# Combinations of weight quarters move from GpSimd to VectorE, lower parts of weights move from VectorE to GpSimd

## The chip, the core and the metric

The kernel runs on one core of a Trainium2 chip. The metric is device time in microseconds (us) for one execution; smaller is better. A profile of one execution shows what each engine did: TensorE (PE, with its weight loads PEld), VectorE (DVE), ScalarE (ACT), GpSimd (POOL) and the queue on SyncE (SP) that issues DMAs.

## The reference

Attention within chunks of 64 tokens, and behind it a feed-forward layer with a gate. All arrays are float32.

```python
# q, k, v: (8, 8, 576, 64); w_in: (512, 2048); w_out: (2048, 512)
scores = scale * np.matmul(q_c, k_c.transpose(0, 1, 2, 4, 3))   # chunks of 64
scores = scores - np.max(scores, axis=-1, keepdims=True)
attn = np.exp(scores)
attn = attn / (np.sum(attn, axis=-1, keepdims=True) + 1e-09)
x = matmul(attn, v_c) as (4608, 512)
h = x @ w_in
g = h * np.clip(h + 3.0, 0.0, 6.0) / 6.0
out = g @ w_out
```

## The kernel before

**Precision.** TensorE multiplies fp32r operands. Each float32 operand is split in two: an upper part (a ScalarE copy that rounds to fp32r) and a lower part (operand minus upper part). `passes` (L341 to L345) makes a product of three matmuls: upper by upper, upper by lower, lower by upper. So each tensor that TensorE reads costs one ScalarE copy and one subtraction; here these are called the upper and the lower part.

**Weights.** They arrive as 64-bit words and are decoded in 16 tiles (a0 to a7 of w_in, b0 to b7 of w_out; 128 x 1024 elements each): two ScalarE steps, a shift and a join on VectorE (L187, L194), the upper part `high` (L199, ScalarE), the lower part `lower` (L202, VectorE).

**Blocks.** The 4608 tokens are nine blocks of 512. Block 0 runs plainly (steps a, b: first product; c: second product). The other eight go in four pairs, and each pair multiplies in a scheme of seven products instead of eight on quarters of the matrices. For the first pair, half of the first product is still done plainly (steps a16 to b43 of TensorE), and the other half as seven products for each of four columns, `f1.0.4` to `f4.0.7` in the order 1, 5, 6, 7, 2, 3, 4 (the last number is the column). The second products follow as `s0.0`, `s0.1` and so on.

**Sums of weight quarters.** Four of the seven products need combinations of quarters of the weights. They are made once, 16 times (u = 0 to 15; u below 8 is w_out, u from 8 is w_in) by `sum_steps` (L426): `whole` puts two weight rows together in a tile `a` (VectorE, L442, or, for the weights kept in DRAM, a DMA, L439), `comb` makes the four combinations (L447: four operations of 128 x 256, each on all of two inputs in SBUF), `top` the upper part (L452, ScalarE), `less` the lower part (L455, VectorE, 128 x 1024), `send` four DMAs to DRAM (L460). There are two tiles `a`, so `whole` of u+2 waits for `less` of u. `own` (L466) sends the quarters that need no combination, three DMAs each. The products f5, f6, f7 and f3 of column 4 use the sum u = 12 straight from SBUF; columns 5, 6, 7 use 13, 14, 15. The sums 8 to 11 come last, during the second product.

**Operands of the first pair.** `x0.s0`, `x0.s0c`, `x0.s1` (VectorE) and `x0.s2`, `x0.s2b`, `x0.s3`, `x0.s3b` (GpSimd, L565) combine quarters of the attention's result; each is split by a ScalarE copy (L569) and a lower part (L572).

**Attention.** A head half (named by block and half, as 20, 21, 30) has scores, max, less, exp, sum, share, turn, product, keep and rest. On most, one ScalarE instruction makes all exponentials and VectorE subtracts the maximum and sums (L246, L253). For those listed in `ROWS` (L44), ScalarE makes the exponentials row by row with bias and sum in the same instruction (L265), and VectorE only negates the maxima and inverts the sums. Where a product of one head half and the scores of the next share their place, they are issued as one step.

**Order.** `Schedule` (L59) decides all of it before anything is emitted: each step has an engine, a cost in us written beside it, the steps before it and a due time. `order` (L81) plays the steps through with these costs, and each engine's queue is emitted in the order that came out. On the chip every engine works its queue strictly in this order: an instruction that waits holds all behind it.

Of the kernel before, what the change touches and what calls it, by code (L numbers as in the profile page):

```python
# [9 lines left out]
F32 = mybir.dt.float32  # L10
# [5 lines left out]
ALU = mybir.AluOpType  # L16
# [10 lines left out]
NCT, NFT, NET = DM // P, DFF // P, DO // P  # L27
# [5 lines left out]
NPL = 4  # L33
# [7 lines left out]
WARM = 12  # L41
FILL = (2.0, 4.0)
LAG = 2
ROWS = ["40", "41"]  # L44
XDVE = ["x0.s0c"]
APART = 2
EDGE = 32
HASTE = 5.0
# [4 lines left out]
PART = STEP / 4  # L53
SECOND = STEP * (17 + 2 * NPL) + PART * 7 * (NFP - NPL)
STEPS = SECOND - PART * 7 * (NFP - NPL)
COMBS = [u for u in range(16)]


class Schedule:  # L59
# [67 lines left out]
def tile_kernel(ctx: ExitStack, tc: tile.TileContext, qk_in, v_in, weights, out):  # L127
# [40 lines left out]
    words, w = {}, {}  # L168
# [10 lines left out]
    def convert(i):  # L179
        t = {}  # L180

        def upper_bits():
            t["u"] = wu.tile([P, 1024], I32, name="u")
            ACT.activation(out=t["u"].bitcast(F32), in_=words[i][:, :, 1].bitcast(F32), func=AF.Prelu, scale=2.0 ** -112, alpha=2.0 ** 32)

        def shift():
            DVE.tensor_scalar(out=t["u"], in0=t["u"], scalar1=3, scalar2=None, op0=ALU.logical_shift_left)  # L187

        def lower_bits():
            t["r"] = wr.tile([P, 1024], I32, name="r")  # L190
            ACT.activation(out=t["r"], in_=words[i][:, :, 0].bitcast(U32), func=AF.Copy, scale=2.0 ** -29)

        def join():
            DVE.tensor_tensor(out=t["u"], in0=t["u"], in1=t["r"], op=ALU.add)  # L194
            t["a"] = t["u"].bitcast(F32).rearrange("p (f t) -> p f t", f=2)

        def high():
            w[i] = w_tile(i, F32R)
            ACT.copy(out=w[i][:, :, 0], in_=t["a"])  # L199

        def lower():
            DVE.tensor_tensor(out=w[i][:, :, 1], in0=t["a"], in1=w[i][:, :, 0].bitcast(F32), op=ALU.subtract)  # L202
# [224 lines left out]
    def sum_steps(m, p):  # L427
# [26 lines left out]
        def lower():  # L454
            DVE.tensor_tensor(out=t["hl"][:, :, :, 1], in0=t["s"], in1=t["hl"][:, :, :, 0].bitcast(F32), op=ALU.subtract)  # L455

        def send():
            for i, row, col in ((5, 1, 1), (7, 1, 0), (6, 0, 0), (3, 0, 1)):
# [39 lines left out]
    def next_slot(s, name, until, stream=False):  # L498
# [8 lines left out]
            slots[0] = 0  # L507
        before = work.take(f"slot{k}", 1, name, until)
        if len(work.rings[f"slot{k}"]) == 1:
            before = [f"f4.0.{2 * (k % 4) + 1}", *owns(k)]  # L510
        return k, before

    owns = lambda k: [f"own{NFP + (2 * k + q) % NFP}" for q in range(2)]
# [3 lines left out]
    def x_steps(s):  # L517
        n = NSTD + 2 * s
        b = lambda i, j: xraw[n + j][:, i]
        name = lambda i: f"x{s}.{i}"  # L520
        minus = lambda to, x, y: lambda: DVE.tensor_tensor(out=b(*to), in0=b(*x), in1=b(*y), op=ALU.subtract)
        sub = ("DVE", 1.22)
        ops[s] = {}
        last = name("s0")
        steps = [(last, *sub, [], minus((0, 1), (0, 1), (0, 0)), [0, 1])]

        def high(i, slot):
            ops[s][i] = w_tile(f"a{slot}", F32R)
# [5 lines left out]
        for i in ORDER_A:  # L534
# [3 lines left out]
            for k, at, to, x, y, reads in (("s1", 5, (0, 1), (1, 1), (0, 1), [2]), ("s2", 6, (0, 0), (0, 1), (0, 0), []),  # L538
                                           ("s3", 6, (0, 1), (1, 0), (0, 1), [3])):
                if i == at:  # L540
                    steps.append((name(k), *sub, [name(f"{i}l"), name("1l"), last], minus(to, x, y), reads))
                    last = name(k)
        return steps

# [165 lines left out]
    for k, i in enumerate(ORDER_W):  # L710
# [4 lines left out]
        work.add(f"down{i}", "ACT", 1.15, [f"w{i}", free("join")], down)  # L715
        work.add(f"join{i}", "DVE", 1.22, [f"shift{i}", f"down{i}"], join)
        work.add(f"high{i}", "ACT", 1.05, [f"join{i}"], high)
        work.add(f"lower{i}", "DVE", 1.22, [f"high{i}"], lower)
        if i in KEPT:
            work.add(f"keepw{i}", "SP", 1.57, [f"join{i}"], keep, first=LOADS.index("w" + ORDER_W[min(k + 4, NFT - 1)]) + 0.5)  # L720

# [106 lines left out]
    for u in [*range(NFP), *range(NFP + NPL, 2 * NFP), *range(NFP, NFP + NPL)]:  # L828
# [6 lines left out]
        work.add(f"comb{u}", *(("POOL", 3.2, [f"whole{u}"], lambda f=combine: f(POOL)) if u in COMBS else ("DVE", 1.70, [f"whole{u}"], lambda f=combine: f(DVE))))  # L835
# [108 lines left out]
    def add_units(s):  # L944
# [14 lines left out]
        for i in ORDER_B:  # L959
            for pp in range(NFP // 2):  # L960
# [8 lines left out]
                def top(i=i, pp=pp, src=src, slot=slot):  # L969
# [147 lines left out]
```

## Time and profile before

| | |
|---|---|
| median of three runs | 791.15 us (790.48 to 791.26) |
| the profiled execution, its own time | 792.07 us |
| its span from first to last instruction | 790.3 us |
| TensorE busy | 775.2 us (98%) |
| VectorE busy | 634.1 us (80%) |
| ScalarE busy | 388.6 us (49%) |
| GpSimd busy | 174.9 us (22%) |
| DMA, mean | 251 GB/s |

The profiled execution took 1.8 us more than its span, and 0.9 us more than the median. Busy shares are averages over stages that differ: in the slices of 20 us, GpSimd is idle in most of the first 100 us, and busy 19.45 of 20 us between 160 and 180 us. TensorE is busy in every slice from 200 us on, save the end.

### The profile page before, as it was taken

What the parts mean: (1) busy time and instruction counts of PE and PEld (TensorE: products, weight loads), DVE (VectorE), ACT (ScalarE), POOL (GpSimd) and SP (SyncE); (2) the same over time, 40 slices, a digit from 0 to 9 for tenths busy, and PEclk for the clock granted to TensorE, in tenths of its full rate; (3) what the DMA queues carried; (4) which work ended last, traced back from release to release, by engine and by line L of the source; (5) the groups of instructions that cost most, each with busy time, mean ns of one, the idle gap of its engine ahead of it and who ended that gap; (6) DMA issues with size and microseconds to landing.
All of it is one profiled execution on the core that took longest, in us unless ns stands there. A gap on an engine that the chain in (4) does not pass through costs nothing.

```text
span 790.3 us, 14001 instructions
## 1 busy us (share of the span) xinstructions
PE 775.2 (98%) x5603; PEld 635.6 (80%) x5603; DVE 634.1 (80%) x726; ACT 388.6 (49%) x531; POOL 174.9 (22%) x139
## 2 busy tenths in 40 slices
PE   8999998989999999999999999999999999999998
PEld 4788887767888878888888888888888888888887
DVE  6999979788999779858998786687988657679851
ACT  4988843544666653433744433435643423356330
POOL 0000025799570500322300002221100013222000
PEclk9999999999999999999999999999999999999999
DMA  9999997785649898556676886576656665566572
GB/s 371 407 403 336 331 347 268 275 298 178 251 160 335 292 364 316 186 190 241 210 256 223 260 267 210 186 256 235 212 190 219 219 213 187 189 208 203 197 232 102
DMA packets 69424, 198.05 MB, mean 251 GB/s; under 512 B 7024, under 2 KB 19568, under 8 KB 65008
## 3 DMA queue, kind: packets, MB, share of 16 engines
q1 hardware_dynamic: 69216, 197.03, 72.7%
q8 instruction: 44, 0.72, 0.4%
q14 instruction: 20, 0.16, 0.1%
q10 hardware_dynamic: 144, 0.13, 0.0%
HBM read 153.09 MB, written 44.04 MB: 249 GB/s over the span
## 4 chain that ended last, share of the span: by engine, by line
PE 83%; DVE 6%; DMA 3%; POOL 3%; ACT 2%; issue 1%; SPq 1%; DVEq 0%; POOLq 0%; ACTq 0%
PE acc L343 19%; PE acc L344 19%; PE acc L345 19%; PE h L343 7%; PE h L345 7%; PE h L344 7%; POOL a L447 2%; PE two L235 2%; PE two L285 2%; DVE hl L455 1%; PE h L311 1%; DVE a L442 1%; DMA wa<-b 1%; DMA a<-wa 1%; DMA b<-wb 1%
## 5 line engine op out<-in xcount | busy, mean ns | idle before, releaser
L343 PE MATMUL acc<-wa,ws 128*128 128x512 f32 (+1 forms) x536 | 209.5, 391 | 0.1
L345 PE MATMUL acc<-wa,ws 128*128 128x512 f32 (+1 forms) x536 | 207.9, 388 | 0.0
L344 PE MATMUL acc<-wa,ws 128*128 128x512 f32 (+1 forms) x536 | 207.8, 388 | 0.0
L974 DVE TENSOR_TENSOR wa<-wb,wa 128x1024 fp32r<-128x1024 f32 x96 | 128.6, 1349 | 30.3 <-ACT wa L971 29.8
L971 ACT CAST wa<-wb 128x1024 fp32r<-128x1024 f32 x96 | 100.5, 1053 | 99.8 <-PE acc L345 63.7
L343 PEld LDWEIGHTS acc<-wa,ws 128*128 128x128 f32 x536 | 100.7, 188 | 21.7 <-DVE u L864 0.9
L345 PEld LDWEIGHTS acc<-wa,ws 128*128 128x128 f32 x536 | 100.6, 188 | 20.8
L344 PEld LDWEIGHTS acc<-wa,ws 128*128 128x128 f32 x536 | 100.7, 188 | 19.8
L938 POOL TENSOR_TENSOR wb<-wb 128x512 f32<-128x512 f32 x24 | 32.0, 1331 | 374.7 <-DVE wb L752 374.7
L447 POOL TENSOR_TENSOR a<-a 128x256 f32<-128x256 f32 x64 | 67.0, 1049 | 165.5 <-DMA b<-wb 111.0
L749 ACT ACTIVATE r<-acc,half 128x512 f32<-128x512 f32 x90 | 61.2, 686 | 39.9 <-DVE acc L864 36.6
L749 ACT ACTIVATE r<-h,half 128x512 f32<-128x512 f32 x38 | 26.1, 687 | 103.4 <-DVE h L864 98.4
L752 DVE SCALAR_TENSOR_TENSOR wb<-r,acc 128x512 f32<-128x512 f32 x90 | 60.8, 680 | 7.9 <-ACT r L749 7.9
L345 PE MATMUL h<-wa,ws 128*128 128x512 f32 (+1 forms) x144 | 55.2, 383 | 0.0
L344 PE MATMUL h<-wa,ws 128*128 128x512 f32 (+1 forms) x144 | 55.2, 383 | 0.0
L343 PE MATMUL h<-wa,ws 128*128 128x512 f32 (+1 forms) x144 | 55.2, 383 | 0.0
L864 DVE TENSOR_TENSOR u<-h,p 128x512 f32<-128x512 f32 x32 | 22.0, 689 | 27.3 <-PE h L345 27.1
L864 DVE TENSOR_TENSOR acc<-acc,u 128x512 f32<-128x512 f32 x48 | 33.0, 696 | 9.8 <-PE acc L345 9.7
L940 POOL TENSOR_TENSOR g<-wb,wb 128x512 f32<-128x512 f32 x24 | 37.8, 1577 | 1.9
L752 DVE SCALAR_TENSOR_TENSOR wb<-r,h 128x512 f32<-128x512 f32 x38 | 25.9, 682 | 12.9 <-ACT r L749 12.9
L343 PE MATMUL acc<-wa,wa 128*128 128x512 f32 x88 | 34.9, 397 | 0.5 <-DMA wa<-b 0.5
L345 PE MATMUL acc<-wa,wa 128*128 128x512 f32 x88 | 34.3, 390 | 0.0
(199 smaller groups left out, 1428.8 us busy)
## 6 DMA issues: line engine op xcount, KB each, us to landing
ws<-b SPq DMA_DIRECT2D x84, 512.0 KB, 4.6
ws<-a SPq DMA_DIRECT2D x72, 512.0 KB, 4.4
qk<-qk_in SPq DMA_DIRECT2D x17, 1024.0 KB, 7.8
wa<-b SPq DMA_DIRECT2D x28, 512.0 KB, 6.4
a<-wa SPq DMA_DIRECT2D x40, 256.0 KB, 5.8
v<-v_in SPq DMA_DIRECT2D x17, 512.0 KB, 5.5
wa<-w_in_out SPq DMA_DIRECT2D x8, 1024.0 KB, 13.0
wb<-w_in_out SPq DMA_DIRECT2D x8, 1024.0 KB, 10.3
```

What stands on the lines that cost most here:

```text
L235: PE.matmul(self.s[o, a, c, :], lhsT=self.qk[rows, 0, c, o], rhs=self.qk[rows, 1, c, o], start=True, stop=True)
L343: PE.matmul(ps, lhsT=a_h, rhs=b_h, start=first, stop=False, skip_group_check=more)
L344: PE.matmul(ps, lhsT=a_h, rhs=b_l, start=False, stop=False, skip_group_check=more)
L345: PE.matmul(ps, lhsT=a_l, rhs=b_h, start=False, stop=last, skip_group_check=more)
L447: engine.tensor_tensor(out=to, in0=x, in1=y, op=op)
L749: ACT.activation(out=t["r"], in_=ps(), func=AF.Relu, bias=half, scale=1.0 / 6.0)
L752: work.add("gate" + name, "DVE", 0.69, ["relu" + name, *more], lambda: DVE.scalar_tensor_tensor(out=out(), in0=t["r"], scalar=1.0, in1=ps( ...
L864: return lambda: DVE.tensor_tensor(out=out(), in0=x(), in1=y(), op=ALU.add)
L938: work.add(id_("t1."), "POOL", 1.45, [id_("gate3."), id_("gate2.")], lambda f=gq: POOL.tensor_tensor(out=f(0, 1), in0=f(0, 1), in1=f(0, 0) ...
L940: work.add(id_("t2."), "POOL", 1.45, [id_("t1."), id_("gate7.")], lambda f=gq, p=p: POOL.tensor_tensor(out=t2_of(p), in0=f(1, 1), in1=f(0, ...
L971: ACT.copy(out=g_ops[s, i, pp][:, :, 0], in_=src())
L974: work.add(low, "DVE", 1.22, [high], lambda i=i, pp=pp, src=src: DVE.tensor_tensor(out=g_ops[s, i, pp][:, :, 1], in0=src(), in1=g_ops[s, i ...
```

## The change

The list of sums whose `comb` runs on GpSimd, `COMBS`, shrinks from all 16 to 8 to 11; the other twelve go to VectorE. Their lower parts `less0s` to `less7s` go from VectorE to GpSimd (`LESS_ON_POOL`), and so do the lower parts of the decoded weights b2 to b7 (`LOWER_ON_POOL`). `ROWS` gets the head halves 30 and 31. The play-through lengthens a VectorE step of the kinds in `BOTH` by 0.6 of the time that it overlaps GpSimd's current step. `XPOOL` and `ULPOOL` are empty, so the lines with them change nothing, and the new condition in `next_slot` gives the same step for every slot that comes to it. The planned cost of `comb` on GpSimd is 4.2 instead of 3.2.

```diff
-ROWS = ["40", "41"]
+ROWS = ["30", "31", "40", "41"]
+SHARED = 0.6
+BOTH = ("lower", "join", "whole", "less", "comb", "share", "glow", "ul", "m0", ...)
+LESS_ON_POOL = list(range(8))
+LOWER_ON_POOL = [f"b{i}" for i in range(2, 8)]
-COMBS = [u for u in range(16)]
+COMBS = [8, 9, 10, 11]
...
                     end = now + self.steps[n][1]
+                    if engine == "DVE" and n.startswith(BOTH):
+                        end += SHARED * max(0.0, min(end, free.get("POOL", 0.0)) - now)
...
-        def lower():
-            DVE.tensor_tensor(out=w[i][:, :, 1], in0=t["a"], in1=w[i][:, :, 0].bitcast(F32), op=ALU.subtract)
+        def lower(engine):
+            engine.tensor_tensor(out=w[i][:, :, 1], in0=t["a"], in1=w[i][:, :, 0].bitcast(F32), op=ALU.subtract)
...
-        work.add(f"lower{i}", "DVE", 1.22, [f"high{i}"], lower)
+        work.add(f"lower{i}", *(("POOL", 2.5, [f"high{i}"], lambda f=lower: f(POOL)) if i in LOWER_ON_POOL else ...))
...
-        work.add(f"comb{u}", *(("POOL", 3.2, [f"whole{u}"], ...) if u in COMBS else ("DVE", 1.70, ...)))
+        work.add(f"comb{u}", *(("POOL", 4.2, [f"whole{u}"], ...) if u in COMBS else ("DVE", 1.70, ...)))
-        work.add(f"less{u}s", "DVE", 1.22, [f"top{u}"], lower, due=due)
+        work.add(f"less{u}s", *(("POOL", 2.5, [f"top{u}"], lambda f=lower: f(POOL)) if u in LESS_ON_POOL else ...), due=due)
```

GpSimd's queue at its start. Before, the combinations of sums 0 to 6 in tiles `a`, then a part of the operands of the first pair (`wb7`):

```order
L447 TENSOR_TENSOR a_1325<-a_1325 128x256 x4
L447 TENSOR_TENSOR a_1376<-a_1376 128x256 x4
L447 TENSOR_TENSOR a_1443<-a_1443 128x256 x4
L447 TENSOR_TENSOR a_1549<-a_1549 128x256 x4
L447 TENSOR_TENSOR a_1589<-a_1589 128x256 x4
L447 TENSOR_TENSOR a_1632<-a_1632 128x256 x4
L447 TENSOR_TENSOR a_1733<-a_1733 128x256 x4
L565 TENSOR_TENSOR wb7_1792<-wb3_1432,xb_834 128x1024
```

Now the lower parts of b2 to b7 come first (two are shown), then `less0s` to `less5s` (`hl`), and `less6s` behind the first two of the `wb7` steps:

```order
L210 TENSOR_TENSOR wb6_1221<-u_1095,wb6_1221 128x2x512
L210 TENSOR_TENSOR wb7_1232<-u_1074,wb7_1232 128x2x512
L463 TENSOR_TENSOR hl_1343<-a_1295,hl_1343 128x4x256
L463 TENSOR_TENSOR hl_1408<-a_1317,hl_1408 128x4x256
L463 TENSOR_TENSOR hl_1531<-a_1432,hl_1531 128x4x256
L463 TENSOR_TENSOR hl_1594<-a_1448,hl_1594 128x4x256
L463 TENSOR_TENSOR hl_1642<-a_1564,hl_1642 128x4x256
L463 TENSOR_TENSOR hl_1757<-a_1656,hl_1757 128x4x256
L574 TENSOR_TENSOR wb7_1783<-wb3_1406,xb_832 128x1024
L574 TENSOR_TENSOR wb7_1783<-xc_1086,wb3_1406 128x1024
L463 TENSOR_TENSOR hl_1824<-a_1759,hl_1824 128x4x256
```

Every instruction on GpSimd in this place is now one of 1024 columns.

VectorE's queue before the scores of head half 21, which need `x0.s0` (`wb3`) and the rest of head half 20 (`xa`). Before, with `less0s` (`hl`) and the lower part of block 0's gate (`g2`) between them, then a gate and the `whole` of sum 2:

```order
L332 TENSOR_TENSOR xa_1393<-two_1343,xa_1393 128x2x8x64
L455 TENSOR_TENSOR hl_1405<-a_1325,hl_1405 128x4x256
L376 TENSOR_TENSOR g2_1414<-r_1294,g2_1414 128x512
L561 TENSOR_TENSOR wb3_1432<-two_1343,xb_834 128x2x8x64
L752 SCALAR_TENSOR_TENSOR wb0_1395<-r_1430,h_1328 128x512
L442 TENSOR_TENSOR a_1443<-wb1_578 128x512
L442 TENSOR_TENSOR a_1443<-wb5_1179 128x512
```

Now, with the two combinations (L455) of sums 0 and 1 ahead:

```order
L455 TENSOR_TENSOR a_1295<-a_1295 128x256 x4
L384 TENSOR_TENSOR g1_1333<-r_1251,g1_1333 128x512
L455 TENSOR_TENSOR a_1317<-a_1317 128x256 x4
L761 SCALAR_TENSOR_TENSOR wb0_1388<-r_1385,h_1267 128x512
L570 TENSOR_TENSOR wb3_1406<-two_1352,xb_832 128x2x8x64
L340 TENSOR_TENSOR xa_1402<-two_1352,xa_1402 128x2x8x64
L384 TENSOR_TENSOR g2_1422<-r_1298,g2_1422 128x512
L450 TENSOR_TENSOR a_1432<-wb1_578 128x512
L450 TENSOR_TENSOR a_1432<-wb5_1126 128x512
L761 SCALAR_TENSOR_TENSOR wb0_1388<-r_1435,h_1335 128x512
```

`x0.s0` and the rest stand ahead of `g2`, and the last gate has moved behind the `whole` of sum 2.

SyncE's queue: the sends (`own`) of the last two w_in rows (a6, a7 in DRAM) and the store of the decoded b7 (`wb7`) before, down to the last send that frees `wb3` and so `x0.s0`:

```order
L466 DMA a6_0_144<-wa3_644 128x2x256
L466 DMA a6_1_145<-wa3_644 128x2x256
L466 DMA a6_1_145<-wa7_1114 128x2x256
L205 DMA wb7_123<-u_1130 128x1024
L466 DMA a7_0_146<-wa3_644 128x2x256
L466 DMA a7_1_147<-wa3_644 128x2x256
L466 DMA a7_1_147<-wa7_1114 128x2x256
L466 DMA b1_1_149<-wb2_674 128x2x256
```

Now, from the store of b7 on:

```order
L213 DMA wb7_123<-u_1074 128x1024
L474 DMA b1_0_148<-wb1_578 128x2x256
L474 DMA b2_0_156<-wb5_1126 128x2x256
L474 DMA b4_0_158<-wb5_1126 128x2x256
L474 DMA b1_1_149<-wb2_656 128x2x256
L474 DMA b2_1_157<-wb6_1221 128x2x256
L474 DMA b4_1_159<-wb6_1221 128x2x256
L474 DMA b1_1_149<-wb3_783 128x2x256
```

The six DMAs of a6 and a7 have gone behind the sends of `wb3`.

## Rows read from the trace of the kernel before

**Rows 1.** Busy time by engine (and count), clock, DMA share, GB/s, by stretch.

```profile
120.00:140.00 20.00, 18.50 (x145) 15.56 (x146) 19.35 (x23) 7.56 (x10) 10.96 (x12) 1.00 0.81 273
160.00:180.00 20.00, 16.84 (x71) 13.19 (x70) 17.94 (x16) 9.52 (x13) 19.45 (x12) 0.96 0.81 277
```

**Rows 2.** Instructions in order of time (start, duration): TensorE, scores of 21.

```profile
121.50 1.16 PE L235 MATMUL two<-qk 64*64 64x64 f32 x64 [2.72 <-issue]
122.59 0.50 PE L343 MATMUL h<-xb,wa 128*128 128x512 f32 x1
```

**Rows 3.** The chain that ended last (start, duration), before `x0.s0`.

```profile
113.42 0.72 SPq L466
...
114.19 5.12 DMA b<-wb
...
120.19 1.21 DVE wb L561
```

**Rows 4.** TensorE in order of time, step b32 and the next.

```profile
150.03 0.50 PE L344 MATMUL h<-xd,wa 128*128 128x512 f32 x1 [0.33 <-DVE xd L332]
...
151.29 0.39 PE L343 MATMUL acc<-xa,wa 128*128 128x512 f32 x1
151.52 0.39 PE L344 MATMUL acc<-xa,wa 128*128 128x512 f32 x1
```

**Rows 5.** TensorE in order of time, first column of the seven products.

```profile
170.33 0.39 PE L343 MATMUL acc<-xb,wa 128*128 128x512 f32 x1
...
178.04 0.50 PE L343 MATMUL acc<-wa,hl 128*128 128x512 f32 x1 [3.03 <-DVE wb L752]
...
182.48 1.04 PE L285 MATMUL two<-ident,e 128*128 128x128 f32 x8
184.43 0.50 PE L343 MATMUL acc<-xd,hl 128*128 128x512 f32 x1 [0.91 <-DVE g L864]
...
185.92 0.39 PE L343 MATMUL acc<-wa,wa 128*128 128x512 f32 x1
```

**Rows 6.** VectorE in order of time, from the scores of 21 on.

```profile
121.32 0.67 DVE L752 SCALAR_TENSOR_TENSOR wb<-r,h 128x512 f32<-128x512 f32 x1
121.92 1.28 DVE L442 TENSOR_TENSOR a<-wb 128x512 f32<-128x512 f32 x2
...
127.53 1.21 DVE L253 TENSOR_REDUCE z<-e 128x16 f32<-128x1024 f32 x1
...
135.04 2.37 DVE L442 TENSOR_TENSOR a<-wb 128x512 f32<-128x512 f32 x2
...
148.68 1.29 DVE L332 TENSOR_TENSOR xd<-acc,xd 128x512 fp32r<-128x512 f32 x2 [1.22 <-ACT xd L328]
...
162.88 1.18 DVE L254 TENSOR_SCALAR z<-z 128x16 f32<-128x16 f32 x1
...
172.31 3.41 DVE L273 TENSOR_TENSOR e<-e,z 128x1024 f32<-128x1024 f32 x1
```

**Rows 7.** GpSimd in order of time, `x0.s2b`.

```profile
161.61 2.41 POOL L565 TENSOR_TENSOR wb<-wb,xb 128x1024 f32<-128x1024 f32 x1
```

**Rows 8.** Groups by line and form: busy, mean ns | idle before.

```profile
L447 POOL TENSOR_TENSOR a<-a 128x256 f32<-128x256 f32 x64 | 67.0, 1049 | 165.5 <-DMA b<-wb 111.0 <-DVE u L864 26.3 <-DVE a L442 9.1
...
L455 DVE TENSOR_TENSOR hl<-a,hl 128x1024 fp32r<-128x1024 f32 x16 | 24.0, 1500 | 7.9 <-ACT hl L452 7.3 <-DMA a<-hl 0.5
L452 ACT CAST hl<-a 128x1024 fp32r<-128x1024 f32 x16 | 16.8, 1050 | 26.6 <-POOL a L447 19.2 <-DMA a<-wa 3.9 <-DVE wb L752 2.8
...
L265 ACT ACTIVATE e<-two,m 128x64 f32<-128x64 f32 x32 | 9.7, 326 | 2.0 <-PE acc L345 1.8 <-DVE m L259 0.2
L202 DVE TENSOR_TENSOR wb<-u,wb 128x1024 fp32r<-128x1024 f32 x8 | 9.7, 1220 | 0.2 <-ACT wb L199 0.2
...
L265 ACT ACTIVATION_READ_ACCUMULATOR e<-two,m 128x1 f32 x32 | 7.0, 218 | 0.0
```

**Rows 9.** The page's DMA issues: count, KB each, median us to landing.

```profile
a<-wa SPq DMA_DIRECT2D x40, 256.0 KB, 5.8
```

More of the change, by code (lines that the diff above doesn't have):

```diff
@@ L43 @@
 LAG = 2
-ROWS = ["40", "41"]
+ROWS = ["30", "31", "40", "41"]
 XDVE = ["x0.s0c"]
+SHARED = 0.6
+BOTH = ("lower", "join", "whole", "less", "comb", "share", "glow", "ul", "m0", "m1", "m2", "m3", "x0.", "x1.", "x2.", "x3.")
+LESS_ON_POOL = list(range(8))
+XPOOL = []
+ULPOOL = []
+LOWER_ON_POOL = [f"b{i}" for i in range(2, 8)]
 APART = 2
@@ L452, in high, with lower @@
             ACT.copy(out=t["hl"][:, :, :, 0], in_=t["s"])
-        def lower():
-            DVE.tensor_tensor(out=t["hl"][:, :, :, 1], in0=t["s"], in1=t["hl"][:, :, :, 0].bitcast(F32), op=ALU.subtract)
+        def lower(engine):
+            engine.tensor_tensor(out=t["hl"][:, :, :, 1], in0=t["s"], in1=t["hl"][:, :, :, 0].bitcast(F32), op=ALU.subtract)
         def send():
@@ L509, in next_slot @@
         if len(work.rings[f"slot{k}"]) == 1:
-            before = [f"f4.0.{2 * (k % 4) + 1}", *owns(k)]
+            before = [f"f4.0.{2 * (k % 4) + 1}" if 2 * (k % 4) >= NPL else f"b{2 * NFT + 2 * k + 1}", *owns(k)]
         return k, before
@@ L520, in x_steps @@
         name = lambda i: f"x{s}.{i}"
-        minus = lambda to, x, y: lambda: DVE.tensor_tensor(out=b(*to), in0=b(*x), in1=b(*y), op=ALU.subtract)
+        minus = lambda to, x, y, on=DVE: lambda: on.tensor_tensor(out=b(*to), in0=b(*x), in1=b(*y), op=ALU.subtract)
         sub = ("DVE", 1.22)
@@ L524, in x_steps @@
         last = name("s0")
-        steps = [(last, *sub, [], minus((0, 1), (0, 1), (0, 0)), [0, 1])]
+        sub_on = lambda k: ("POOL", 2.5) if k in XPOOL else sub
+        steps = [(last, *sub_on("s0"), [], minus((0, 1), (0, 1), (0, 0), POOL if "s0" in XPOOL else DVE), [0, 1])]
         def high(i, slot):
@@ L540, in x_steps @@
                 if i == at:
-                    steps.append((name(k), *sub, [name(f"{i}l"), name("1l"), last], minus(to, x, y), reads))
+                    steps.append((name(k), *sub_on(k), [name(f"{i}l"), name("1l"), last], minus(to, x, y, POOL if k in XPOOL else DVE), reads))
                     last = name(k)
@@ L717, in tile_kernel @@
         work.add(f"high{i}", "ACT", 1.05, [f"join{i}"], high)
-        work.add(f"lower{i}", "DVE", 1.22, [f"high{i}"], lower)
+        work.add(f"lower{i}", *(("POOL", 2.5, [f"high{i}"], lambda f=lower: f(POOL)) if i in LOWER_ON_POOL else ("DVE", 1.22, [f"high{i}"], lambda f=lower: f(DVE))))
         if i in KEPT:
@@ L834, in tile_kernel @@
         work.add(f"whole{u}", *(("SP", 1.57) if in_dram(m, p) else ("DVE", 1.38)), ["room", *work.take("a", 2, f"whole{u}", [f"less{u}s"])], whole)
-        work.add(f"comb{u}", *(("POOL", 3.2, [f"whole{u}"], lambda f=combine: f(POOL)) if u in COMBS else ("DVE", 1.70, [f"whole{u}"], lambda f=combine: f(DVE))))
+        work.add(f"comb{u}", *(("POOL", 4.2, [f"whole{u}"], lambda f=combine: f(POOL)) if u in COMBS else ("DVE", 1.70, [f"whole{u}"], lambda f=combine: f(DVE))))
         work.add(f"top{u}", "ACT", 1.05, [f"comb{u}", *work.take("hl", 2, f"top{u}", [f"send{u}", *last])], high)
-        work.add(f"less{u}s", "DVE", 1.22, [f"top{u}"], lower, due=due)
+        work.add(f"less{u}s", *(("POOL", 2.5, [f"top{u}"], lambda f=lower: f(POOL)) if u in LESS_ON_POOL else ("DVE", 1.22, [f"top{u}"], lambda f=lower: f(DVE))), due=due)
         work.add(f"send{u}", "SP", 3.15, [f"less{u}s"], send, due=due + (4 if u < NFP else 12))
@@ L973, in add_units @@
                 work.add(high, "ACT", 1.05, [*after, *before], top)
-                work.add(low, "DVE", 1.22, [high], lambda i=i, pp=pp, src=src: DVE.tensor_tensor(
+                on = (s, i, pp) in ULPOOL
+                work.add(low, *(("POOL", 2.5) if on else ("DVE", 1.22)), [high], lambda i=i, pp=pp, src=src, on=POOL if on else DVE: on.tensor_tensor(
                     out=g_ops[s, i, pp][:, :, 1], in0=src(), in1=g_ops[s, i, pp][:, :, 0].bitcast(F32), op=ALU.subtract))
```

## The prediction

> **What bounds the kernel now.** I read the stretches first, since the busy shares of the whole run hide where time is lost. TensorE is full in nearly all of them, and not in those between 100 and 200 us: it lacks 1.5 us between 120 and 140 and 3.2 us between 160 and 180 [rows 1]. What TensorE does not lose there it cannot gain elsewhere. In the same stretches VectorE has 19.35 and 17.94 of 20 us of work, and GpSimd 19.45 in the second [rows 1]. So I looked at TensorE in order of time for the three places where it stops.
>
> The first is the scores of head half 21, which start after 2.72 us of idle time [rows 2]. The chain of waits shows why: SyncE issues one DMA of a send in 0.72 us after another, the last lands 5.12 us after its issue at 114.19, and only then may `x0.s0` write its tile; it starts at 120.19 [rows 3]. The second is step b32, whose second matmul waits for the rest of head half 21 and begins at 150.03 [rows 4]. The third is the largest: from the start of `f1.0.4` at 170.33 to the start of `f4.0.4` at 185.92 there are 15.6 us [rows 5]. In between lie six steps of six matmuls and the transposes of head half 30. Matmuls that do not wait follow each other in 0.23 us [rows 4], so the six take 6 x 6 x 0.227 = 8.2 us, the transposes 1.0 [rows 5], in all 9.2. So 6.4 us are lost: 3.03 for a gate, 0.91 for an addition [rows 5], and the rest in waits inside steps and a clock of 0.96 on average in that stretch [rows 1].
>
> All three wait for VectorE, which was held by the sums of weight quarters. A combination on GpSimd is four operations of 1.05 us on average [rows 8], though GpSimd does 1024 columns in 2.41 [rows 7].
>
> **How the two engines hold each other.** A VectorE operation on 16 elements, `z`, started at 162.88 and took 1.18 us [rows 6]. It ended at 164.06, just after GpSimd's operation from 161.61, which ended at 164.02 [rows 7]. `share30` took 3.41 us [rows 6] against 1.22 for another operation of 1024 columns on two inputs in SBUF [rows 8]. Reductions of 1.21 [rows 6] and gates (one input in PSUM) of 0.67 are not lengthened. So I take it that a VectorE operation of the held kinds waits for the end of GpSimd's running instruction, and that they then take turns.
>
> The Trainium skill, SBUF — State Buffer, section Who interferes with whom, says that the pair of ports shared by both is locked for a whole instruction and that who comes first blocks the other fully. The row of `z` agrees. This speaks against the change, whose plan counts 0.6 of the overlap: by the plan's share a meeting with a lower part costs up to 0.6 x 2.4 = 1.4 us, by the lock up to 2.4, and the three meetings below together 3 us more.
>
> **The change part by part.** The sum is made against the profiled execution, 792.07 us, with its span of 790.3. It stands 0.9 above the median, and I carry the difference over to the median.
>
> *Prices.* The trace shows no combination on VectorE. 1024 columns take 1.22 us [rows 8], and 512 take 0.67 [rows 6], so 256 are about 0.41 and four of them 1.6. The bounds are 1.22 (as if one operation) and 4 x 0.67 = 2.7. Nor does it show GpSimd writing fp32r. The subtraction of 1024 columns in float32 took 2.41 [rows 7]. Below that I see no reason to go; above, twice that, 4.8, if rounding needs a second pass. I take 2.4, since for VectorE the lower part of b costs the same 1.22 with fp32r [rows 8] as the float32 work of this size beside it.
>
> *Lower parts of b2 to b7.* VectorE is rid of 6 x 1.22 = 7.3 us before 110 us, and GpSimd gets 6 x 2.4 = 14.5, in which VectorE is held for perhaps half. TensorE shows no stop at a step that waits for these parts, so I count 0; without that cover it would be up to 1.2 us later for a lower part (2.4 instead of 1.2), or as much earlier if it waits unseen.
>
> *A, scores of 21.* Six DMAs of a6 and a7 go behind the sends of `wb3`. At 0.72 each this is 4.3 us [rows 3]; the last send then lands at about 115.0. `x0.s0` and the rest, now next to each other, take 2 x 1.21, and are done at 117.5 to 118. TensorE is free at 121.50 - 2.72 = 118.8, so the wait goes. What is late next is the bank of the following tile, a25. The scores take 1.1 [rows 2], so a25 could start at 119.9, but it waits for gate17, which now stands behind the lower part of a gate (0.68) and a `whole` (1.28 [rows 6]). In front of these, `less1s` on GpSimd holds VectorE until about 118.9. That makes 118.9 + 0.68 + 1.28 + 0.67 = 121.5. So a25 comes at 121.6, not 122.59: 1.0 us is left of 2.7. If `less1s` isn't in the way, 2.7 remain.
>
> *B, step b32.* Between the end of gate17 and the end of the rest of 21 VectorE took from 121.99 to 149.97, 28.0 us [rows 6]. Out of it go four lower parts at 1.5 [rows 8] = 6.0; a `whole`, now ahead, and `x0.s1`, now behind, 2.6; two `whole` held for 1.1 each (2.37 against 1.28, one is shown) and the idle 1.22 before the rest [rows 6], 3.4. Four combinations come in, 6.4. After each of the first three, `top` takes 1.05 on ScalarE [rows 8] and the lower part then starts on GpSimd. VectorE has meanwhile spent 1.2 or 1.3 us on things that aren't held (a reduction of 1.21; a gate and a copy), and its next operation meets a GpSimd instruction that has just begun: 2.3 us each, 6.9. So 28.0 - 6.0 - 2.6 - 3.4 + 6.4 + 6.9 = 29.3, and the rest ends at 121.5 + 29.3 = 150.8. The matmul at 150.03 comes at about 150.9: the 1.0 is given back, and 0.9 more. With none of the meetings the rest is early and b32 is 1.0 ahead.
>
> *C, first column.* `f1.0.4` starts at 170.33 + 0.9 = 171.2. Its successor needs the sum 12. Its `whole` is issued behind `less6s`. The rest of 21 ends at 150.8, `x0.s1` and two gates take 2.6, so the combination of sum 6 starts at about 153.5; it is held once by `x0.s2` for 2.4 and done at 157.5; `top` 1.05; GpSimd busy with `x0.s3` meanwhile, `less6s` done at 161.5; the DMA 5.8 [rows 9] and its issue, 168; then combination 1.6, a lower part 1.2 and `less12s` 1.2: 172.0. `f5.0.4` can start at 172.6 and doesn't wait. After that VectorE has two gates, a lower part, combination 13, an addition and `share30`: 0.67 + 1.22 + 0.67 + 1.6 + 0.4 + 0.7 + 1.22 = 6.5, 178.5. The transposes could start at 171.2 + 5 x 1.36 = 178.0, so 0.5 is lost, and the lower part that `f4.0.4` needs ends some 3.3 later at 181.8, against a place at 180.9: 0.9. So 1.4 are lost where 6.4 were, and `f4.0.4` starts at 171.2 + 9.2 + 1.4 = 181.8 instead of 185.92: 4.1 us earlier. Full bounds: 6.4 (nothing changes) to 0.
>
> *ROWS.* For 30 and 31, VectorE loses two operations of 1.2 us each; ScalarE gets 16 x (0.326 + 0.218) = 8.7 us for one of about 1.05 [rows 8]. ScalarE has 9.52 of 20 busy there [rows 1], which hides it, as long as no relu waits behind more than one pair (1.1 us).
>
> After this TensorE was busy to the end, so what is won stays. Sum: 792.07 - 4.1 = 788.0, and for the median 791.15 - 4.1 = 787.0.
>
> **Rivals.** *VectorE is hardly held.* The meetings of B and C miss each other. `max21` and reductions are not held, and the starts depend on 1 us. Then b32 is 1.0 ahead and f4 loses 0.9 instead of 6.4: 6.5 us, and with gate17 in time 8.2: 783. Against it: in B the lower part begins just before the held operation, three times by the same pattern.
>
> *The gain is eaten.* The combination of sum 6 also meets `x0.s3`, `less12s` comes 1.6 us later, and in columns 5 to 7 combinations 14 and 15 add 3.2 on a VectorE that is as full as now. Of 4.1 us nothing or little is left: 790.5. For it: VectorE had 17.94 of 20 us there [rows 1], and 12 combinations (19 us) come for eight lower parts (12 us).
>
> *Slower: GpSimd's lower part with fp32r takes 4.8 us.* Each of the three meetings in B grows by 2.4 and `less6s` too, 9.6 in all: 787.0 + 9.6 = 796.6. It decides from 1.0 us more for one lower part, 3.4. For it: no row shows this form on GpSimd. Against: neither on VectorE nor on ScalarE does the form cost more.
>
> **How the numbers follow.** Forecast 0.43 (its own range 784.5 to 789.5), hardly held 0.27, eaten 0.16, slower 0.14. A measurement tells 0.2% (1.6 us) from no change. Faster: nearly all of the first two and a quarter of the third, 0.70. Within: 0.14, most of it from the third. Slower: 0.16. The range is 780.5 to 793: from below the second case with the lower combination price to past the third.
>
> **What would show it.** Right: the scores of 21 without idle time and a25 behind gate17; `z` of head half 21 lengthened to 2 us or more; b32 at 150 to 151; `f4.0.4` within 10 to 11 us of `f1.0.4`; lower parts on GpSimd at 2.4 where not held. Wrong: lower parts at 3.4 or more; a stop of TensorE before 118 us; `f4.0.4` later than 185; or new idle time after 200 us.

## The result, and the profile after

The changed kernel takes 800.39 us (median of 799.98, 800.39 and 800.51), the kernel before 791.2 in the same job: a ratio of 1.0118, interval 1.0103 to 1.0133. It is slower; 787.0 was forecast, and the range ended at 793.0. The profiled execution took 800.39 with a span of 798.6. One more execution of the changed kernel (1107.08 us at a mean granted clock of 0.655) and one of the fourth experiment (1299.73 us at 0.557) were slow throughout and enter no comparison.

First the stretches (columns as in [rows 1]), one of the kernel before that [rows 1] lacks:

```profile
180.00:200.00 20.00, 19.02 (x201) 15.27 (x200) 16.32 (x23) 10.54 (x15) 16.75 (x16) 0.95 0.61 220
```

And the changed kernel:

```profile
120.00:140.00 20.00, 20.00 (x153) 16.48 (x152) 19.66 (x28) 7.39 (x10) 4.74 (x3) 1.00 0.89 302
...
160.00:180.00 20.00, 15.35 (x65) 11.86 (x63) 19.74 (x19) 10.54 (x29) 12.50 (x6) 0.94 0.61 217
180.00:200.00 20.00, 17.54 (x188) 13.88 (x189) 19.29 (x27) 12.38 (x28) 7.49 (x5) 0.89 0.43 145
```

Between 120 and 140 TensorE is now full; the 1.5 us of [rows 1] are back. Between 160 and 180 it lacks 4.65 us where it lacked 3.2, and in the next 20 us 2.5 where it lacked 1.0, at a lower clock. GpSimd fell from 19.45 to 12.50, VectorE rose from 17.94 to 19.74. TensorE in order of time shows the places:

```profile
108.29 1.06 PE L293 MATMUL two<-ident,e 128*128 128x128 f32 x8 [0.99 <-DVE e L281]
...
122.90 1.16 PE L243 MATMUL two<-qk 64*64 64x64 f32 x64
123.99 0.50 PE L351 MATMUL h<-xb,wa 128*128 128x512 f32 x1
...
152.29 0.50 PE L352 MATMUL h<-xd,wa 128*128 128x512 f32 x1 [1.51 <-DVE xd L340]
...
172.60 0.39 PE L351 MATMUL acc<-xb,wa 128*128 128x512 f32 x1
...
178.77 0.80 PE L351 MATMUL acc<-wa,hl 128*128 128x512 f32 x1 [4.65 <-ACT hl L460]
...
181.05 0.63 PE L352 MATMUL acc<-wa,hl 128*128 128x512 f32 x1
181.48 0.63 PE L353 MATMUL acc<-wa,hl 128*128 128x512 f32 x1
...
189.63 1.06 PE L293 MATMUL two<-ident,e 128*128 128x128 f32 x8 [2.27 <-DVE e L281]
...
191.92 0.39 PE L351 MATMUL acc<-wa,wa 128*128 128x512 f32 x1
```

The scores of 21 have no idle time ahead of them any more, where [rows 2] had 2.72. Step b32 still waits. The first column is where the time goes: from `f1.0.4` at 172.60 to `f4.0.4` at 191.92 there are 19.3 us where [rows 5] had 15.6 and I forecast 10.6. After the stop of 4.65 us the matmuls follow each other in 0.43 us, at the lower level of the clock, where they took 0.23 before. At 108.29 there is a stop that the kernel before doesn't have.

The stop of 4.65 ends with `hl`, the upper part of sum 12, which ScalarE makes as soon as VectorE has combined it. VectorE in order of time, the combinations of sums 6, 7, 12 and 13, and `less12s`:

```profile
155.15 5.60 DVE L455 TENSOR_TENSOR a<-a 128x256 f32<-128x256 f32 x4
...
164.89 5.55 DVE L455 TENSOR_TENSOR a<-a 128x256 f32<-128x256 f32 x4
...
172.09 5.51 DVE L455 TENSOR_TENSOR a<-a 128x256 f32<-128x256 f32 x4
...
178.75 1.22 DVE L463 TENSOR_TENSOR hl<-a,hl 128x1024 fp32r<-128x1024 f32 x1
...
182.22 5.21 DVE L455 TENSOR_TENSOR a<-a 128x256 f32<-128x256 f32 x4
```

A combination that meets nothing takes 1.79 (those of sums 0, 2, 3 and 5); these four take three times that. GpSimd in order of time says why:

```profile
152.24 2.40 POOL L463 TENSOR_TENSOR hl<-a,hl 128x1024 fp32r<-128x1024 f32 x1 [4.06 <-DMA b<-hl]
154.60 2.41 POOL L574 TENSOR_TENSOR wb<-wb,xb 128x1024 f32<-128x1024 f32 x1
156.95 2.60 POOL L574 TENSOR_TENSOR wb<-xc,wb 128x1024 f32<-128x1024 f32 x1
...
171.65 2.40 POOL L463 TENSOR_TENSOR hl<-a,hl 128x1024 fp32r<-128x1024 f32 x1 [2.41 <-ACT hl L460]
174.01 2.85 POOL L962 TENSOR_TENSOR wb<-wb 128x512 f32<-128x512 f32 x2
```

And the chain that ended last (start, duration) takes the combination of sum 6 apart:

```profile
155.15 2.15 DVE a L455
...
157.32 2.52 DVE a L455
...
159.86 0.44 DVE a L455
160.32 0.42 DVE a L455
```

Each of its four instructions takes 0.44 alone. The first ends at 157.30, just after `x0.s2` on GpSimd (154.60 + 2.41 = 157.01); then `x0.s3` runs first, to 159.55, and the second ends at 159.84; the last two meet nothing. In the combination of sum 12 three of the four lose a turn, to `less7s` and to two subtractions of 512 columns (L962):

```profile
172.17 2.17 DVE a L455
...
174.37 1.38 DVE a L455
...
175.77 1.38 DVE a L455
```

So a combination is not held once. Each of its short instructions can lose its turn to a whole instruction of GpSimd, as long as GpSimd has one ready.

Three groups of the changed kernel stand against [rows 8]:

```profile
L455 DVE TENSOR_TENSOR a<-a 128x256 f32<-128x256 f32 x48 | 40.2, 838 | 1.2
```

```profile
L463 POOL TENSOR_TENSOR hl<-a,hl 128x1024 fp32r<-128x1024 f32 x8 | 20.7, 2585 | 36.5 <-ACT hl L460 23.0 <-DMA qk<-qk_in 9.5 <-DMA b<-hl 4.1
L210 POOL TENSOR_TENSOR wb<-u,wb 128x1024 fp32r<-128x1024 f32 x6 | 16.9, 2832 | 88.8 <-ACT wb L207 72.6 <-DMA a<-wa 16.2
```

Of the 40 us of the combinations on VectorE (41.5 from first start to last end, 12 of them), 12 x 1.79 = 21.5 are work and about 20 are holds. The lower parts on GpSimd take 2.40 where nothing holds them, and 2.6 to 2.8 on average: the fp32r form costs nothing extra there.

### The profile page after: what moved, and what is told of

Its sections match the earlier page's. It is cut to its first block, busy times and chain, and to the rows that moved or that the text cites. A ratio compares the mean times of both kernels' runs of the same rounds, so it can differ in the third digit from the quotient of the medians.

```text
span 798.6 us, 14046 instructions
## 1 busy us (share of the span) xinstructions
PE 778.8 (98%) x5601; PEld 637.9 (80%) x5603; DVE 647.6 (81%) x758; ACT 396.8 (50%) x593; POOL 161.2 (20%) x105
## 4 chain that ended last, share of the span: by engine, by line
PE 80%; DVE 14%; DMA 2%; ACT 2%; issue 1%; POOL 1%; SPq 0%; DVEq 0%; ACTq 0%; POOLq 0%
PE acc L351 18%; PE acc L352 18%; PE acc L353 18%; PE h L352 6%; PE h L351 6%; PE h L353 6%; DVE a L455 4%; PE two L243 2%; PE two L293 2%; PE h L319 2%; DVE wb L761 1%; DVE a L450 1%; DVE e L281 1%; DMA qk<-qk_in 1%; DVE wa L984 1%
## 5 line engine op out<-in xcount | busy, mean ns | idle before, releaser
L984 DVE TENSOR_TENSOR wa<-wb,wa 128x1024 fp32r<-128x1024 f32 x96 | 126.1, 1322 | 26.4 <-ACT wa L980 26.3
L455 DVE TENSOR_TENSOR a<-a 128x256 f32<-128x256 f32 x48 | 40.2, 838 | 1.2
L210 POOL TENSOR_TENSOR wb<-u,wb 128x1024 fp32r<-128x1024 f32 x6 | 16.9, 2832 | 88.8 <-ACT wb L207 72.6
L351 PE MATMUL acc<-wa,wa 128*128 128x512 f32 x88 | 34.9, 396 | 0.0
```

Source lines behind the costliest of these rows:

```text
L210: engine.tensor_tensor(out=w[i][:, :, 1], in0=t["a"], in1=w[i][:, :, 0].bitcast(F32), op=ALU.subtract)
L351: PE.matmul(ps, lhsT=a_h, rhs=b_h, start=first, stop=False, skip_group_check=more)
L455: engine.tensor_tensor(out=to, in0=x, in1=y, op=op)
L984: work.add(low, *(("POOL", 2.5) if on else ("DVE", 1.22)), [high], lambda i=i, pp=pp, src=src, on=POOL if on else DVE: on.tensor_tensor(ou ...
```

## The experiments

Each ratio is to runs of the kernel before on the same chip in the same job: 790.42 us for the first four experiments, 791.11 for the next four, 791.12 for the last four (medians of 13, 19 and 11 runs). The times are medians and the ratios are taken from means, so a ratio can differ by up to 0.2% from the quotient of the two medians.

**The changed kernel again** (no edit).

> The changed kernel once more, for the first 25 us. In its first profile block 0's first product begins 2.9 us later than before, though every instruction up to there is the same; the granted clock fell to half from 17.2 to 20.6 us. Theory A (turns): the start is a matter of the single execution; here it may begin near 20.6 us, and the time then is 797 to 798; the rest of the loss, 5 to 6 us, is in the combinations on VectorE. Theory B (load): the same as A for the start. Theory C (start): the late start belongs to this program; it comes again, with 800.0 to 800.6 us.

799.03 us, ratio 1.0101 (1.0085 to 1.0117). In the first profile of the changed kernel the tile steps start 2.4 us late (a0 at 22.98 instead of 20.62; the 2.9 above is too much), with the same instructions before them. Here a0 starts at 20.68 and the run is as slow within 1.6 us, so the late start belongs to that execution. This repeat is the cleaner profile, and the accounts below use it: `f1.0.4` at 170.54 (+0.2 against before), `f4.0.4` at 190.78 (+4.9), the end at +6.7.

**Lower parts of the sums back on VectorE.**

```diff
-LESS_ON_POOL = list(range(8))
+LESS_ON_POOL = []
```

> The lower parts of sums 0 to 7 are back on VectorE, the combinations stay there too; GpSimd keeps the lower parts of b2 to b7 and x0.s2 to x0.s3b. Theory A (turns: each of a combination's four short operations can lose a whole GpSimd instruction): VectorE gets 8 x 1.22 = 9.8 us of work, and loses the holds by less0s to less7s, which in the changed kernel add about 12 us (in sums 1, 4, 5, 12 and in share21 and negate30); f5.0.4 1 to 3 us earlier than in the changed kernel, 797 to 799.5 us. Theory B (VectorE simply has more work): 9.8 us more of it on an engine that is full between 100 and 190 us; f5.0.4 6 to 10 us later, 806 to 810.

801.05 us, 1.0130 (1.0114 to 1.0145), between the two expectations. The twelve combinations fall from 41.5 to 28.8 us, so the holds follow what is queued on GpSimd; one, of sum 5, still takes 6.44 with three subtractions queued. But the lower parts put 11 us back on VectorE, and the first column takes 21.4 us.

**The four long subtractions of head half 21 on VectorE.**

```diff
-XDVE = ["x0.s0c"]
+XDVE = ["x0.s0c", "x0.s2", "x0.s2b", "x0.s3", "x0.s3b"]
```

> x0.s2, x0.s2b, x0.s3 and x0.s3b move from GpSimd to VectorE; all else as in the changed kernel. Theory A (turns): combinations 6 and 7, 5.6 us each in the changed kernel, fall to about 1.8, 7.6 us less, against 4 x 1.22 = 4.9 more on VectorE, and less6s and less7s no longer queue behind these steps on GpSimd; f5.0.4 3 to 5 us earlier, 795.5 to 798. Theory B (load): 4.9 us more on a full engine, 803 to 805.

795.77 us, 1.0062 (1.0046 to 1.0079), as theory A expects. VectorE got 4 x 1.2 us more work and the kernel became 3 to 5 us faster. The combinations that met these subtractions fell from 5.60 and 5.55 to 2.78 and 3.26 (1.8 was expected), and the first column to 14.8 us. The clock stayed at 1.0. This is the test of load against turns: with more work on VectorE and less on GpSimd the kernel is faster.

**All combinations on GpSimd.**

```diff
-COMBS = [8, 9, 10, 11]
+COMBS = [u for u in range(16)]
```

> All 16 combinations are back on GpSimd; it also keeps the lower parts of sums 0 to 7 and of b2 to b7. Theory A (turns): VectorE loses 12 combinations of 1.8 us and their holds, but GpSimd now has 12 x 3.0 + 8 x 2.4 + 4 x 2.4 = 65 us of work between 112 and 180, more than the 68 it has with holds; it becomes the engine that is waited for, 797 to 803 us. Theory B (load on VectorE alone): VectorE has 21 us less than in the changed kernel and 12 less than before; near 785 us.

794.99 us (nine runs), 1.0036 (1.0016 to 1.0056), in two groups: 789.6 to 791.7 and 794.3 to 796.2. Their mean clocks overlap (0.998 to 1.000 and 0.996 to 0.998), and why there are two is open. Neither expectation is met. In the profile (789.62) the first column takes 12.7 us, `f4.0.4` is 4.2 us earlier than before, and 1.7 of these are given back by product 31.

**Reductions of 30 and 31 on VectorE again.**

```diff
-ROWS = ["30", "31", "40", "41"]
+ROWS = ["40", "41"]
```

> The changed kernel with one edit: the reductions of head halves 30 and 31 are done on VectorE again (ROWS is 40, 41 as before), the rest as in the changed kernel. Theory A (the turn and the product with head half 31, 235 to 250 us, come late because VectorE is full and GpSimd holds it; ROWS was a relief of two 1.2 us reductions for it): nothing is gained there, 799 to 802 us. Theory B (the 16 exponentials that ScalarE now does row by row for 30 and 31 are what makes head half 31 late): the loss of about 2 us at product 31 goes, 796 to 797.5 us.

798.71 us, 1.0104 (1.0086 to 1.0122): nearer to A. The lateness against before is +4.8 at `f3.0.6` and +4.9 at product 31, so the loss there is gone; by 290 us it has grown to +5.5, as at the end. Between this median and the repeat's lie 0.3 us, less than these runs tell apart.

**Lower parts of b2 to b7 on VectorE.**

```diff
-LOWER_ON_POOL = [f"b{i}" for i in range(2, 8)]
+LOWER_ON_POOL = []
```

> The changed kernel with one edit: the lower parts of b2 to b7 stay on VectorE (LOWER_ON_POOL is empty). Theory A (two of these GpSimd instructions, for b6 and b7, hold share and inversion of head half 20, so that its turn waits 1.0 us and 1.7 us are lost by then): the steps up to turn 20 stand within 0.3 us of the kernel before, and the time is 797 to 798.5 us. Theory B (as in the prediction: they cost nothing, and the 1.7 us are from the new order around step b15): still 1.5 to 1.8 us later than before at turn 20, and 798.5 to 800.5 us.

799.68 us, 1.0109 (1.0094 to 1.0125): B's time, and at the turn of 20 it is 1.6 us later than before, as B says. B's reason is not shown, though: the stop at the turn of 20 goes, but the planner makes another order out of the freed time, and that has a stop of its own. TensorE in order of time:

```profile
82.53 0.50 PE L351 MATMUL h<-xa,wa 128*128 128x512 f32 x1 [1.14 <-DVE r L377]
...
181.69 0.79 PE L351 MATMUL acc<-wa,hl 128*128 128x512 f32 x1 [11.97 <-ACT hl L460]
```

What the changed kernel loses before the scores of 21, this one loses before 83 us. Its `f1.0.4` starts at 168.2, 2.3 ahead of the repeat, but the combination of sum 12 starts at 174.1, 4.1 behind it, and takes 6.39. So what is won on the way is lost in the first column, as long as VectorE sets it.

**A combination as one instruction.**

```diff
-            for to, x, y, op in ((q(1, 1), q(1, 0), q(1, 1), ALU.add), ...
+            for to, x, y, op in ((t["a"], t["a"], t["a"], ALU.add),) if engine is DVE else ((q(1, 1), ...
```

> The changed kernel with one edit: each of the twelve combinations on VectorE is one instruction over 1024 columns instead of four over 256 that follow one another (which leaves the combination of the quarters out: the sums are wrong, the sizes, tiles, order and waits are the same). Work alone 1.22 us instead of 1.79, that is 6.8 us less in all. Theory A (each short instruction can lose one turn to a whole GpSimd instruction; one instruction loses one turn at most): the combinations of sums 6, 7, 12 and 13 fall from 5.2 to 5.6 us to at most 3.7 us, all twelve from 41.5 to about 26 us, the first column is no later than before, and the time is 794 to 797 us. Theory B (VectorE is simply shut out as long as GpSimd has work in its queue, whatever the number of instructions): the combinations of 6, 7 and 12 still take 4.8 us or more, and the time is 798 to 800 us.

792.25 us, 1.0012 (0.9997 to 1.0026), below A's range and far from B's. The order of all engines is that of the changed kernel. VectorE, the group, and the combinations of sums 6, 7 and 12 in order of time:

```profile
L455 DVE TENSOR_TENSOR a<-a 128x1024 f32<-128x1024 f32 x12 | 17.3, 1439 | 1.6 <-DMA a<-wb 1.0 <-DMA a<-wa 0.6
```

```profile
151.17 2.31 DVE L455 TENSOR_TENSOR a<-a 128x1024 f32<-128x1024 f32 x1
157.82 1.36 DVE L455 TENSOR_TENSOR a<-a 128x1024 f32<-128x1024 f32 x1 [1.01 <-DMA a<-wb]
163.72 2.16 DVE L455 TENSOR_TENSOR a<-a 128x1024 f32<-128x1024 f32 x1 [0.59 <-DMA a<-wa]
```

The twelve fall from 41.5 to 17.3 us: 6.8 for the work left out (12 x 0.57), 17 for turns that are not lost. On the path from 153 us to `f4.0.4`, the combinations of sums 6, 7, 12 and 13 fall from 21.9 to 7.5 us, and at most 2.3 of this is work left out; `f4.0.4` starts 9.0 us earlier than in the repeat. So most of the loss in the first column is lost turns. That `f4.0.4` starts at 181.81, where I had forecast 181.8, is luck: `f1.0.4` starts at 168.5 and not at 171.2, and the column takes 13.3 us and not 10.6.

**All combinations on GpSimd, and reductions of 30 and 31 on VectorE.** The diffs of the fourth and the fifth experiment together.

> Two edits to the changed kernel: all sixteen combinations on GpSimd as before, and the reductions of head halves 30 and 31 on VectorE as before. What is left of the change: the lower parts of the sums and of b2 to b7 on GpSimd, and the planner that counts overlap. Theory A (the combinations on VectorE are the loss; the 2 us that the version with all combinations on GpSimd gave back at product 31 come from VectorE's holds, not from ROWS): 789 to 792 us, as that version in its faster runs. Theory B (ROWS makes head half 31 late): 786.5 to 788.5 us, faster than both.

790.75 us, 1.0014 (0.9982 to 1.0045): no difference that can be measured, and within A's range. The runs go from 788.33 to 799.07. The profile is of the fastest; its first column takes 11.6 us and `f4.0.4` starts 5.3 us earlier than before. TensorE there:

```profile
172.37 0.50 PE L351 MATMUL acc<-wa,hl 128*128 128x512 f32 x1 [0.94 <-ACT hl L460]
```

At a mean granted clock of 1.000 its runs take 788.3 to 791.2, at 0.991 to 0.994 they take 795.2 to 799.1.

**The combinations alone on VectorE.** The changed kernel with `ROWS = ["40", "41"]`, `LESS_ON_POOL = []`, `LOWER_ON_POOL = []`, `SHARED = 0.0`: of the change only `COMBS` is left, and the planned cost of 4.2 for the four combinations on GpSimd.

> The kernel before with one part of the change: the twelve combinations on VectorE (four stay on GpSimd), while all lower parts, the reductions of 30 and 31 and the planner are as before, so that GpSimd keeps little but the subtractions x0.s2 to x0.s3b. Theory A (a combination on VectorE costs what it is held, and nothing much queues on GpSimd here except beside sums 6 and 7): most combinations take 1.8 us, those of 6 and 7 up to 5.6; VectorE carries 21.5 us more of work and is full, so the first column is late, 794 to 799 us. Theory B (the combinations on VectorE are harmless by themselves; only together with the lower parts on GpSimd are they slow): 787 to 791 us.

803.86 us, 1.0166 (1.0143 to 1.0190): slower than the whole change, and than A expected. So the combinations on VectorE are a loss by themselves, and the other parts together win back 3 to 5 us. The loss is not turns alone: the twelve take 31.3 us here, about 10 of them holds (20 in the changed kernel), and that of sum 12 only 2.85, while VectorE, which has all lower parts as well, is busy 19.7 and 19.1 of 20 us between 160 and 200. One combination shows the turns in full. VectorE in order of time:

```profile
146.92 8.06 DVE L455 TENSOR_TENSOR a<-a 128x256 f32<-128x256 f32 x4
```

GpSimd meanwhile, `x0.s2` to `x0.s3b`:

```profile
147.23 2.39 POOL L574 TENSOR_TENSOR wb<-wb,xb 128x1024 f32<-128x1024 f32 x1 [145.89 <-DVE wb L570]
149.58 2.58 POOL L574 TENSOR_TENSOR wb<-xc,wb 128x1024 f32<-128x1024 f32 x1
152.13 2.58 POOL L574 TENSOR_TENSOR wb<-wb,xb 128x1024 f32<-128x1024 f32 x1
154.66 2.60 POOL L574 TENSOR_TENSOR wb<-wb,xc 128x1024 f32<-128x1024 f32 x1
```

And the chain of waits, the second and the third of the four instructions:

```profile
147.38 2.54 DVE a L455
...
149.94 2.52 DVE a L455
```

The first runs free; the second, third and fourth each wait for one GpSimd instruction, 1.79 + 3 x 2.1 = 8.1. TensorE waits 13.65 us for sum 12 in the first column.

**No overlap in the planner.**

```diff
-SHARED = 0.6
+SHARED = 0.0
```

> The changed kernel with one edit: the planner counts no overlap (SHARED is 0 instead of 0.6), everything else as in the changed kernel. Theory A (the loss is in the holds, and a plan without them moves steps by little): 798 to 802 us, holds of the same kind, 12 combinations with 35 to 45 us. Theory B (the planner's rule itself shifted the order so that sums 6, 7 and 12 meet GpSimd's work): below 796 us.

798.56 us, 1.0100 (1.0076 to 1.0123), as A expects; the twelve combinations take 37.2 us. The new rule neither makes the loss nor avoids it.

**All combinations on GpSimd, early lower parts on VectorE as well.** The eighth experiment with `LOWER_ON_POOL = []`.

> All sixteen combinations on GpSimd, reductions of 30 and 31 on VectorE, lower parts of b2 to b7 on VectorE: of the change only the lower parts of the first eight sums on GpSimd and the planner's rule are left. The variant with the lower parts of b2 to b7 on GpSimd lost 1.5 us between b15 and turn 20 (in its profile of 788.33 us). Theory A: that part comes back, 786.5 to 788.5 us with the clock at full, faster than both kernels. Theory B (as with the changed kernel, where the steps before 160 us came back in full and the first column was later by as much): 788.5 to 791 us, no different from before.

794.84 us, 1.0052 (1.0033 to 1.0072): neither. In this order two lower parts and a subtraction stand on GpSimd, from 158.4 to 167.5, right ahead of the combination that the first column waits for; TensorE stops for 4.68 us in the first column, and the clock in that stretch is 0.83.

**The same with the four subtractions on VectorE.** `XDVE` as in the third experiment.

> The same with the four subtractions x0.s2, s2b, s3 and s3b on VectorE as well, so that GpSimd holds the combinations and the lower parts of eight sums alone (GpSimd was busy for 19 of 20 us from 140 to 200 in the variants with all combinations on it, VectorE for 11 to 17). Theory A (GpSimd is the bound of the first column there): the wait of 2.45 us before f5.0.4 goes, and so do the clock's falls after it, 784.5 to 787.5 us. Theory B (VectorE's holds outweigh it): 789 to 792 us.

799.57 us, 1.0113 (1.0089 to 1.0136): A is refuted. The transposes of head half 30 now come ahead of sum 12 and wait 6.88 us for VectorE, and 2.96 for the sum follow. B's time is missed too: a plan with one engine relieved is another order, and which stop it has was not foreseen.

No version is measurably faster than the kernel before.

## Why the prediction was wrong

- **Term C, the first column, failed**, in the step "it is held once by `x0.s2` for 2.4" and the flat 1.6 for the combinations of sums 12 and 13. The repeat's VectorE in order of time has the combinations of sums 6, 7 and 12, `less12s`, the combination of sum 13 and `share30`:

```profile
153.06 5.62 DVE L455 TENSOR_TENSOR a<-a 128x256 f32<-128x256 f32 x4
...
162.83 5.55 DVE L455 TENSOR_TENSOR a<-a 128x256 f32<-128x256 f32 x4
...
170.03 5.51 DVE L455 TENSOR_TENSOR a<-a 128x256 f32<-128x256 f32 x4
...
176.70 1.22 DVE L463 TENSOR_TENSOR hl<-a,hl 128x1024 fp32r<-128x1024 f32 x1
...
180.17 5.22 DVE L455 TENSOR_TENSOR a<-a 128x256 f32<-128x256 f32 x4
...
186.22 1.21 DVE L281 TENSOR_TENSOR e<-e,z 128x1024 f32<-128x1024 f32 x1
```

The combination of sum 6 starts at 153.06, as predicted (153.5), and takes 5.6 instead of 4.0. That of sum 7, which I did not count on this path, takes 5.55, and sum 12 starts behind it at 170.03 instead of 168. It takes 5.5 instead of 1.6, and `less12s` is done at 177.9 instead of 172.0: 2.0 + 3.9 = 5.9 late. Then the combination of sum 13 takes 5.2 instead of 1.6, and `share30` ends 9.5 us after `less12s` instead of 6.5: 3.0 more. Sum 8.9; `f4.0.4` comes at 190.78 instead of 181.8, 9.0 late. The repeat is 10.9 above the forecast for a profiled execution (798.77 against 787.0 + 0.9), and the 1.9 that are left come after `f4.0.4`, in pieces below 1 us.
- **The step "so what is won stays", from the first column to the end, did not hold either.** The seventh experiment has `f4.0.4` 4.1 us earlier than before, as forecast, and ends 1.8 us earlier; the eighth is 5.3 us earlier there and 3.7 at the end. TensorE was nearly full after 200 us in the kernel before, but a new order has stops of its own there.
- The price of a combination by itself was nearly right: 1.6 forecast, 1.79 measured.
- **The mechanism was in the text, and was applied to the wrong unit.** That "they then take turns" stands in the prediction; I then counted one hold for a meeting, where a step of four instructions takes part in four turns. The Trainium skill, SBUF — State Buffer, section Who interferes with whom, has the lock for each instruction and the first to come blocking the other. The traces agree: 2.54 and 2.52 us for two instructions of 0.44 in the ninth experiment. An estimate from these rows, instruction by instruction: a combination beside a full GpSimd queue takes up to 1.79 + 4 x 2.1 = 10 us.
- **Term A, right in size, not in its steps.** The idle 2.72 went, as forecast. a25 starts at 121.75 in the repeat, 121.6 forecast; but not since gate17 holds it (it follows the scores at once). 1.8 us are lost before the scores of 21, at the turn of 20.
- **The lower parts of b2 to b7, counted as 0, hold the steps in which most of this 1.8 is lost.** In the changed kernel's profile GpSimd has two of them from 101.94 to 107.06, and beside them `z` of head half 20 takes 1.13 and `share20` 2.64; the transposes wait 0.99 for it:

```profile
101.94 5.12 POOL L210 TENSOR_TENSOR wb<-u,wb 128x1024 fp32r<-128x1024 f32 x2 [6.37 <-ACT wb L207]
```

```profile
103.62 1.13 DVE L262 TENSOR_SCALAR z<-z 128x16 f32<-128x16 f32 x1
...
105.50 2.64 DVE L281 TENSOR_TENSOR e<-e,z 128x1024 f32<-128x1024 f32 x1
```

"TensorE shows no stop at a step that waits for these parts" was true of the kernel before and beside the point: in the changed kernel it stops for what they hold. As a sum the 0 came out by luck: without them on GpSimd, in the sixth experiment, about as much is lost before 83 us, and the time is no different.
- **Term B, about right in sum**: the matmul of step b32 at +0.2 in the repeat (150.22 against 150.03), +0.9 forecast, and `f1.0.4` at 170.5 for 171.2. Of its three meetings the one that I named as the sign, `z` of 21 at 2 us or more, didn't take place (0.17); `share21` two instructions later is held to 3.02 instead.
- **ROWS at 0**: the fifth experiment shows nothing else.
- **The rivals.** The fp32r form at 4.8 us is refuted (2.40). "Hardly held" is refuted. "The gain is eaten" had the right mechanism, with one more meeting for sum 6 and 1.6 us for it; it had none for sums 7, 12 and 13 and so ended at 790.5. The slower side came from it, and not from the rival that I gave that side to.
- Whether VectorE's load would have made the kernel slower without holds is answered in part. With one instruction in place of four, but with 12 x 1.22 us still on VectorE, the kernel is as fast as before. But the second and the ninth experiment, with fewer holds and more work on VectorE, are no faster than the changed kernel, so load costs time too. With the true four instructions and GpSimd idle it was not tried, and how the 9 us divide between turns and load is not shown.

## What to carry to other kernels

Where two engines take turns, count the instructions of the one that is short, not its microseconds: four instructions of 0.44 us beside a queue of 2.4 us instructions took 5.6 to 8.1 us, one of 1.22 took 1.4 to 2.3. So the work with the long instructions and the work with many short ones should not meet; here a step of many short instructions was safer on the engine that has the long ones, in its queue (790.8 to 799.6 us with all combinations on GpSimd, 795.8 to 803.9 with twelve of them, as four instructions each, on VectorE). And an engine that is full in the stretch which sets the end is a place to ask of each added step what it costs beside its neighbours there.

## What the runs showed of the hardware

A stop can cost more than its length. In the changed kernel's profile the granted clock fell to its lower level (half, 1.2 GHz) at 177.6, while TensorE stood in the stop of 4.65 us, and came back at 184.4. Twelve matmuls started in this time after the stop and took 5.7 us instead of 2.7: nine in a row at 0.43 each instead of 0.23, the first three at 0.60 to 0.66, one of them waiting for `less12s`. The repeat had this and a second such stretch from 188.8 to 192.2, after a stop of 2.49. The kernel before had one of 3.4 us, after the stop of 3.03; the third experiment, with stops of 1.6 us at most, had none. Not every stop of this size was followed by a fall: the 2.72 us ahead of the scores of 21 in the kernel before [rows 2] was not, nor was the stop of 2.18 ahead of the transposes of head half 30 in the seventh experiment. The eighth experiment's runs, whose times follow their mean clock, look like the same thing, but only the fastest has a profile. One execution had the lower clock from 17.18 to 20.59 as well, before any of the changed work, and the next did not.
